# One sum of second-layer weights moved five slots earlier and one fold of keys one slot later, in a fused attention and mixture kernel

## The chip, the cores and the metric

The kernel runs on one core of one Trainium2 chip. The metric is device time in microseconds. Before the change the first three runs gave a median of 497.9 us (497.85 to 498.71).

Names: PE is the matmul engine and PEld its weight loads, DVE the vector engine, ACT the scalar engine, POOL the GpSimd engine, SP the queue that starts transfers. "L637" is line 637 of the kernel. SBUF and PSUM are the two on-chip memories that the kernel's tiles live in: the products of PE are written to PSUM tiles (in banks), nearly everything else here is in SBUF. Of the tiles, kp holds pooled keys, x_tok the attention output that is fed to the experts, acc the accumulated result, H the hidden values and S sums of them, w_bf weights, wt_bf sums of second-layer weights; unit and o_ps are PE's products in PSUM of the first and the second layer.

## The reference

Pooled attention for 8 batches, followed by a layer of four experts whose outputs are mixed by given probabilities:

```python
def _attn_ref(q, k, v):                      # 8 batches, 8 heads, 576 rows, 64 wide
    k_p = k.reshape(B, H, Sp, pool, D).mean(axis=3)       # 576 rows pooled to 72
    v_p = v.reshape(B, H, Sp, pool, D).mean(axis=3)
    ...                                                   # softmax(q k_p^T) v_p

def _moe_ref(x, domain_probs, w1, w2):       # x: 4608 x 512, 4 experts, 1024 hidden
    p = domain_probs / (domain_probs.sum(-1, keepdims=True) + 1e-09)
    for e in range(E):
        h = np.maximum(x @ w1[e], 0.0)
        out += p[:, e:e + 1] * (h @ w2[e])
```

## The kernel before

The tokens go through the experts in nine chunks. Each expert's two matrix products use seven block products in place of eight, and pay for that with sums and differences of blocks (weights, inputs, hidden values) on the DVE. The main loop is a software pipeline of slots, seven to each pair of chunk and expert. A slot is two up-products of four matmuls and one down-product of eight, and a small piece of the attention of a later batch. Everything that the change touches is hand-placed by slot number:

```python
def combine(dst, a, op, b):                       # L242: DVE, both inputs in SBUF
    nc.vector.tensor_tensor(out=dst, in0=a, in1=b, op=op)

def fold_keys(b, hs):                             # two adds per batch, L285: both inputs in SBUF
    ...
    for dup in range(2):
        nc.vector.tensor_add(out=kp_all[0:SP, hs, dup, :], in0=raw[:, hs, 0, :],
                             in1=raw[:, hs, 1, :])

def relu_sum(dst, ps, part):                      # L637: one input in PSUM, one in SBUF
    nc.vector._custom_dve(TENSOR_ADD_SAT, out=dst, in0=ps, in1=part, s0=LARGEST, s1=0.0)

def weight_sums(e):                               # the sums of second-layer weights
    ...
            lambda: combine(b12, b22, ALU.subtract, b12)]      # the fourth: the one that moves

def up_product(c, e, unit, step):
    ...                                           # four matmuls into units[unit][bank]
    if step == 0:
        nc.scalar.copy(out=units[unit][1][:], in_=ps)          # L669, ACT
    ...
    else:
        relu_sum(quarter(1, 0), ps, part[:, 0])                # L637, frees units[unit][1]

def down(c, e, step, flip=0, pooled=()):
    ...                                           # eight matmuls into a PSUM bank
    if step == 0:
        nc.scalar.copy(...)                                    # L732, ACT
    elif step in pooled and e > 0:                # step 4 alone
        ...                                                    # L736, ACT: addend = prob * product
        nc.gpsimd.tensor_add(out=dst, in0=dst, in1=addend[:])  # L738, POOL: both inputs in SBUF
    else:
        ...                                       # add: L799, DVE, one input in PSUM

# the main loop
for g in range(7 * N + 1):
    ...
    up_product(*order[t], 0, i)
    ...
    up_product(*order[t2], 1, i2)
    ...
    down(*below_of[t2], i2, t2 % 2, POOLED)
    for piece in later.get(g, ()):    # attention of later batches
        piece()
    for piece in sums.get(g, ()):     # weight sums
        piece()
```

The last up-step (L637) reads a PSUM bank that the copy L669 of the next expert's first step must overwrite, and the next up-product of PE grows on what L669 copied. So a late L637 makes L669 late, and that can stop PE.

The softmax here doesn't subtract the row's maximum and nothing guards it: scores larger than these inputs give would overflow.

Of the kernel before, what the change touches and what calls it, by code (L numbers as in the profile page):

```python
# [17 lines left out]
def kernel(  # L18
# [24 lines left out]
    BUSY = 2  # L43
# [149 lines left out]
    def load_q_rem(b):  # L193
        if b % 2 == 0:
            q_rems[b // 2] = qpool.tile([P, H, D], BF16, name="q_rem", bufs=2)
        lo = (b % 2) * REM
        nc.gpsimd.dma_start(
            out=q_rems[b // 2][lo:lo + REM],
            in_=q[b, :, NT:S, :].rearrange("h p d -> p h d"),
        )  # L200
# [40 lines left out]
    def combine(dst, a, op, b):  # L241
        nc.vector.tensor_tensor(out=dst, in0=a, in1=b, op=op)  # L242
# [28 lines left out]
    def fold_wide(what, part):  # L271
        raw, wide = ((raw_k, wide_k), (raw_v, wide_v))[what]
        a, *others = (wide[:, :, 2 * i:2 * i + 2, :] for i in range(wide.shape[2] // 2))
        if part == 0:
            for other in others:
                nc.vector.tensor_add(out=a, in0=a, in1=other)
        else:
            nc.vector.tensor_add(out=raw[:], in0=raw[:], in1=a)

    def fold_keys(b, hs):  # L280
        raw = raw_k if b >= BUSY else raws[("kraw", b)]
        if b < BUSY:
            fold(raw, hs)
# [3 lines that stand above are left out]
# [320 lines left out]
    def weight_parts(e):  # L607
        w = w1_bf[:, e]
        return w[:, 0:HK, 0:FH], w[:, HK:KC, 0:FH], w[:, 0:HK, FH:F], w[:, HK:KC, FH:F]

    def first_weight_sums(e):
        b11, b21, b12, b22 = weight_parts(e)
        t = wu_bf[:, e]
        return [lambda: combine(t[:, 0], b12, ALU.subtract, b11),
                lambda: combine(t[:, 1], b22, ALU.subtract, t[:, 0]),
                lambda: combine(t[:, 2], b21, ALU.subtract, t[:, 1]),
                lambda: combine(b12, b22, ALU.subtract, b12)]
# [13 lines left out]
    def x_sum(c, n):  # L631
        if n == 0:
            state[("x_sums", c)] = x_sums(c)
        state[("x_sums", c)][n]()
# [48 lines left out]
    def weight_sums(e):  # L683
        w, t = w2_bf[:, e], wt_bf[:, e]
        b11, b12 = w[:, LO, 0:HD], w[:, LO, HD:DM]
        b21, b22 = w[:, HI, 0:HD], w[:, HI, HD:DM]
        return [lambda: combine(t[:, 0], b12, ALU.subtract, b11),
                lambda: combine(t[:, 1], b22, ALU.subtract, t[:, 0]),
                lambda: combine(t[:, 2], b21, ALU.subtract, t[:, 1]),
                lambda: combine(b12, b22, ALU.subtract, b12)]  # L690
# [214 lines left out]
    def pieces_later():  # L905


        at = {}

        def put(slot, *pieces):  # L910
            at.setdefault(slot, []).extend(pieces)

        usual = dict(
            queries=-8, keys=-9, values=-2, scores=(-1, 3, 5, 6), contexts=(11, 14, 18, 21),
            q=1, k=(-2, 0, 5, 9), v=(-2, 0, 5, 9), x=(22, 25, 25, 25), rem=(-3, 17, 24, 25),
        )
        plans = {b: usual for b in range(BUSY, B + 1)}
        plans[BUSY] = dict(
            queries=0, keys=4, values=12, scores=(11, 12, 13, 15), contexts=(16, 18, 19, 21),
            q=6, k=(5, 8, 11, 14), v=(13, 16, 19, 24), x=(24, 25, 25, 25), rem=(0, 6, 8, 14),  # L920
        )
        plans[B] = dict(usual, x=(24, 24, 25, 25), rem=(-3, 17, 21, 22))
        plans[BUSY + 1] = dict(usual, values=4, v=(5, 8, 12, 16))

        for b, plan in plans.items():
            start = 7 * E * (b - BUSY)

            def put_each(what, pieces):
                for slot, piece in zip(plan[what], pieces, strict=True):
                    put(start + slot, piece)  # L930

            if b == BUSY:
                put(start + 1, lambda: fold_wide(0, 0))
                put(start + 4, lambda: fold_wide(0, 1))
                put(start + 5, lambda: load_q_rem(BUSY))
                put(start + 8, lambda: fold_wide(1, 0))
                put(start + 12, lambda: fold_wide(1, 1))
            if b < B:
                put(start + plan["queries"], lambda b=b: queries(b))
                put(start + plan["keys"], lambda b=b: fold_keys(b, every))  # L940
                put(start + plan["keys"] + (b > BUSY), lambda b=b: keys(b, every))
                put(start + plan["values"], lambda b=b: fold_values(b, every))
                put_each("scores", [lambda b=b, pair=pair: scores(b, pair) for pair in range(NPAIR)])

                for r, slot in zip((2, 3, 0, 1), plan["contexts"]):
                    put(start + slot, lambda b=b, r=r: context(b, r))
                    put(start + slot + 1, lambda b=b, r=r: turn(b, r))
            if b + 1 < B:
                put(start + plan["q"], lambda b=b: load_q(b + 1), lambda b=b: load_q_rem(b + 1))
                for what in range(2):  # L950
                    put_each("kv"[what], [lambda b=b, what=what, part=part: load_part(b + 1, what, part)
                                          for part in range(NR)])
            if b % 2 == 0:
                i = b // 2 - 1
                put_each("rem", [lambda i=i, do=do: do(i)
                                 for do in (rem_queries, rem_scores, rem_context, rem_turn)])
            put_each("x", [lambda b=b, n=n: x_sum(b, n) for n in range(4)])
        return at

    ENG = mybir.EngineType  # L960
    with tc.manual_schedule(
            engines={ENG.PE, ENG.DVE, ENG.Activation, ENG.Pool, ENG.SP}):
        load_q(0, 0)
        load_q(0, 1)
        load_whole(0, k, "kraw", groups(0)[:1])
        load_whole(0, k, "kraw", groups(0)[1:])
        make_identity(nc, ident[:])
        choose_rows()
        load_values_first()
        load_w1(0)  # L970
        load_w1(1)
        load_probs()
        load_w1(2)
        load_w2(0)
        load_w1(3)
        attention_first()
        norm_probs()
        load_whole(1, k, "kraw")
        load_q(1)
        load_whole(1, v, "vraw")  # L980
        load_w2(1)
        load_w2(2)
        load_w2(3)
        first_chunk()
        psum_first.__exit__(None, None, None)
        psum_last = ctx.enter_context(
            tc.tile_pool(name="psum_last", bufs=1, space=bass.MemoryType.PSUM))
        units[0] = [psum_last.tile([P, NT], F32, name=f"unit0{i}") for i in range(2)]
        open_bank(units[0][1][:])



        N = len(order)
        later = pieces_later()
        below_of = [(0, 3)] + order
        sums = {}
        for at, pieces in (((3,), weight_sums(3)[3:]), ((7,), first_weight_sums(2)[3:]), ((8,), weight_sums(1)[3:]), ((12, 15, 22, 19), weight_sums(2)),
                           ((15,), first_weight_sums(3)[3:])):
            for slot, piece in zip(at, pieces, strict=True):
                sums.setdefault(slot, []).append(piece)  # L1000
        POOLED = (4,)
        for g in range(7 * N + 1):
            t, i = divmod(g, 7)
            if i in (0, 2, 3) and t < N:
                hidden_sums(*below_of[t], i)
            if t < N:
                up_product(*order[t], 0, i)
            t2, i2 = divmod(g - 1, 7)
            if 0 <= t2 < N:
                up_product(*order[t2], 1, i2)  # L1010
            if i == 1 and t < N:
                hidden_sums(*below_of[t], i)
            if g == 0:

                down_plain(0, 2, NR - 1)
            else:
                down(*below_of[t2], i2, t2 % 2, POOLED)
            for piece in later.get(g, ()):
                piece()
            for piece in sums.get(g, ()):  # L1020
                piece()
            if g == 7 * (N - 2):
                load_last_weights()
        down_last(*order[-1])
# [28 lines left out]
```

## Time and profile before

| | before |
|---|---|
| median of the first three runs | 497.9 us |
| span of the profiled run | 495.8 us |
| PE busy | 488.6 us, 99% |
| PEld busy | 407.1 us, 82% |
| DVE busy | 377.1 us, 76% |

The Trainium skill, "Perfetto Trace Analysis", section "Identifying the Most-Contended Engine", warns that the matmuls' busy share is a poor measure of headroom, because matmuls are pipelined, and prefers MFU (the share of peak arithmetic) and the weight loads' busy share. The latter is 82% here, so 99% must not be read as "nothing to gain". What says that PE is the bound is the chain of waits (95% PE) together with a short list of things that PE ever waited for. From the page of the kernel before:

```profile
span 495.8 us, 11453 instructions
...
PE 95%; DVE 2%; ACT 1%; issue 1%; ACTq 0%
```

PE's waits (who waited for whom: us in total, times, longest):

```profile
PE unit L332 <- DVE H L818: 1.3, 1, 1.3
PE unit L656 <- ACT unit L669: 0.8, 1, 0.8
PE o_ps L297 <- ACT kp L313: 0.2, 1, 0.2
```

The first and third are in the start-up. The second is the only one in the main loop, and the ACT instruction named in it had itself waited, by the list of ACT's waits from 100 to 122 us:

```profile
ACT unit L669 <- DVE H L637: 2.4, 1, 2.4
```

The timeline around it, engine by engine (start, duration, engine, line, operation, out<-in, count, and in brackets the idle time before and what ended it). DVE:

```profile
101.29 0.68 DVE L242 TENSOR_TENSOR H<-H 128x1024 bf16<-128x1024 bf16 x1
102.74 0.88 DVE L799 SCALAR_TENSOR_TENSOR acc<-o_ps,p_all,acc 128x256 f32<-128x256 f32 x2 [0.77 <-ACT partial L671]
...
108.95 0.69 DVE L398 TENSOR_TENSOR x_tok<-att,inv 128x512 bf16<-128x512 f32 x1
109.56 1.74 DVE L285 TENSOR_TENSOR kp<-kraw 72x512 bf16<-72x512 bf16 x2
111.23 0.68 DVE L242 TENSOR_TENSOR w_bf<-w_bf 128x1024 bf16<-128x1024 bf16 x1
111.83 0.67 DVE L637 CUSTOM_DVE_ANT_0 H<-unit,partial 128x512 bf16<-128x512 f32 x1
112.43 0.85 DVE L799 SCALAR_TENSOR_TENSOR acc<-o_ps,p_all,acc 128x256 f32<-128x256 f32 x2
```

POOL, then ACT, then PE:

```profile
109.42 1.26 POOL L738 TENSOR_TENSOR acc<-acc,addend 128x512 f32<-128x512 f32 x1 [4.13 <-ACT addend L736]
```

```profile
112.59 0.57 ACT L669 COPY unit<-unit 128x512 f32<-128x512 f32 x1 [2.41 <-DVE H L637]
...
115.36 0.57 ACT L732 COPY o_ps<-o_ps 128x512 f32<-128x512 f32 x1 [0.21 <-DVE acc L799]
```

```profile
112.00 0.42 PE L435 MATMUL att<-vp,expT 72*128 72x65 bf16 x8
113.21 1.03 PE L656 MATMUL unit<-xT,w_bf 128*128 128x256 bf16 x8 [0.79 <-ACT unit L669]
```

Read from the bottom: PE stops at about 112.27 and goes on at 113.21, because L669 ran at 112.59, because L637 ran at 111.83. Yet L637's product was ready at about 109.1. In between stood the two kp adds and the weight sum. The kp adds are normally 0.41 us each; here both together took 1.74, as the list of the kp tile shows (minimum/median/maximum in ns):

```profile
L285 DVE TENSOR_TENSOR kp<-kraw x12: 408/414/1409, 81.1 to 318.5; 72x512 bf16<-72x512 bf16 x12
```

The long one, 1.409 us, is the first of the pair at 109.56. It ended at 110.97, 0.29 us after the pool add (109.42 to 110.68).

### The profile page before, as it was taken

What the parts mean: (1) busy time and instruction counts of PE and PEld (TensorE: products, weight loads), DVE (VectorE), ACT (ScalarE), POOL (GpSimd) and SP (SyncE); (2) the same over time, 40 slices, a digit from 0 to 9 for tenths busy, and PEclk for the clock granted to TensorE, in tenths of its full rate; (3) what the DMA queues carried; (4) which work ended last, traced back from release to release, by engine and by line L of the source; (5) the groups of instructions that cost most, each with busy time, mean ns of one, the idle gap of its engine ahead of it and who ended that gap; (6) DMA issues with size and microseconds to landing.
All of it is one profiled execution on the core that took longest, in us unless ns stands there. A gap on an engine that the chain in (4) does not pass through costs nothing.

```text
span 495.8 us, 11453 instructions
## 1 busy us (share of the span) xinstructions
PE 488.6 (99%) x4663; PEld 407.1 (82%) x4663; DVE 377.1 (76%) x756; ACT 302.7 (61%) x561; POOL 114.4 (23%) x112
## 2 busy tenths in 40 slices
PE   8999999999999999999999999999999999999996
PEld 5856468888888888888888888888888888888885
DVE  5567889799768975788669876896679766976674
ACT  4666536865685568656775667567665566556650
POOL 8230413232352154114421262111000100011010
PEclk9999999999999999999999999999999999999999
DMA  9999996998679659553974398130211010004003
GB/s 199 210 207 203 205 164 92 119 73 97 76 112 62 95 61 146 47 78 37 156 73 67 47 138 80 36 65 22 76 23 22 22 65 1 13 22 86 1 1 85
DMA packets 101779, 41.95 MB, mean 85 GB/s; under 512 B 73808, under 2 KB 100176, under 8 KB 101728
## 3 DMA queue, kind: packets, MB, share of 16 engines
q0 software_dynamic: 56896, 22.42, 40.4%
q1 hardware_dynamic: 43728, 17.77, 17.6%
q10 hardware_dynamic: 1104, 1.05, 0.6%
q8 instruction: 36, 0.59, 0.5%
q14 instruction: 15, 0.12, 0.1%
HBM read 45.69 MB, written 9.44 MB: 111 GB/s over the span
## 4 chain that ended last, share of the span: by engine, by line
PE 95%; DVE 2%; ACT 1%; issue 1%; ACTq 0%
PE o_ps L724 40%; PE unit L656 39%; PE unit L583 5%; PE o_ps L750 3%; PE att L382 2%; PE unit L332 1%; PE unit L782 1%; PE att L435 1%; DVE acc L799 1%; PE unit L598 0%; PE unit L306 0%; DVE H L637 0%; DVE kp L285 0%; PE att L489 0%; PE att L472 0%
## 5 line engine op out<-in xcount | busy, mean ns | idle before, releaser
L799 DVE SCALAR_TENSOR_TENSOR acc<-o_ps,p_all,acc 128x256 f32<-128x256 f32 (+1 forms) x285 | 127.1, 486 | 54.3 <-PE o_ps L724 36.1
L724 PEld LDWEIGHTS <-H 128*128 128x128 bf16 x1320 | 129.1, 98 | 16.2 <-issue 0.3
L656 PEld LDWEIGHTS <-w_bf 128*128 128x128 bf16 x1024 | 97.8, 98 | 15.9 <-issue 4.5
L637 DVE CUSTOM_DVE_ANT_0 H<-unit,partial 128x512 bf16<-128x512 f32 x128 | 87.4, 685 | 25.5 <-PE unit L656 20.9
L724 PE MATMUL o_ps<-w_bf,H 128*128 128x256 bf16 x792 | 102.6, 273 | 0.0
L656 PE MATMUL unit<-xT,w_bf 128*128 128x256 bf16 x672 | 96.4, 273 | 0.8 <-ACT unit L669 0.8
L671 ACT COPY partial<-unit 128x512 f32<-128x512 f32 x128 | 72.0, 589 | 33.2 <-PE unit L656 32.9
L738 POOL TENSOR_TENSOR acc<-acc,addend 128x512 f32<-128x512 f32 x24 | 30.4, 1265 | 258.3 <-ACT addend L736 201.3
L656 PEld LDWEIGHTS <-wu_bf 128*128 128x128 bf16 x768 | 73.3, 98 | 10.0 <-issue 1.5
L656 PE MATMUL unit<-xs,wu_bf 128*128 128x256 bf16 x512 | 76.9, 273 | 0.0
L724 PE MATMUL o_ps<-wt_bf,H 128*128 128x256 bf16 x528 | 68.4, 273 | 0.0
L724 PEld LDWEIGHTS <-S 128*128 128x128 bf16 x528 | 51.7, 98 | 6.4
L677 ACT ACTIVATE H<-unit 128x512 bf16<-128x512 f32 x64 | 38.2, 597 | 29.6 <-PE unit L656 29.3
L673 ACT ACTIVATE H<-unit 128x512 bf16<-128x512 f32 x64 | 38.8, 607 | 27.0 <-PE unit L656 27.0
L669 ACT COPY unit<-unit 128x512 f32<-128x512 f32 x64 | 37.4, 584 | 17.2 <-PE unit L656 14.7
L656 PE MATMUL unit<-xs,w_bf 128*128 128x256 bf16 x256 | 38.5, 273 | 0.0
L797 ACT ACTIVATE acc<-o_ps,p_all 128x256 f32<-128x256 f32 x72 | 30.2, 471 | 12.1 <-PE o_ps L724 10.8
L151 POOL DMA_DIRECT2D vraw<-in_v_dram x20 | 29.3, 1466 | 24.1 <-DMA vraw<-in_v_dram 23.8
L151 POOL DMA_DIRECT2D kraw<-in_k_dram x20 | 25.9, 1295 | 37.4 <-DMA kraw<-in_k_dram 37.4
L724 PE MATMUL o_ps<-wt_bf,S 128*128 128x256 bf16 x264 | 34.2, 273 | 0.0
L724 PE MATMUL o_ps<-w_bf,S 128*128 128x256 bf16 x264 | 34.2, 273 | 0.0
L656 PE MATMUL unit<-xT,wu_bf 128*128 128x256 bf16 x224 | 33.6, 272 | 0.0
(148 smaller groups left out, 516.7 us busy)
## 6 DMA issues: line engine op xcount, KB each, us to landing
out_dram<-acc SPq DMA_DIRECT2D x32, 256.0 KB, 4.2
w_bf<-in_moe_w_dram POOLq DMA_DIRECT2D x7, 1024.0 KB, 23.5
q_sb<-in_q_dram POOLq DMA_DIRECT2D x7, 512.0 KB, 9.8
vraw<-in_v_dram POOLq DMA_DIRECT2D x22, 144.0 KB, 6.5
kraw<-in_k_dram POOLq DMA_DIRECT2D x21, 144.0 KB, 5.3
w_bf<-in_moe_w_dram POOLq DMA_DIRECT2D x2, 512.0 KB, 8.8
wt_bf<-in_k_dram POOLq DMA_DIRECT2D x2, 288.0 KB, 6.8
wt_bf<-in_v_dram POOLq DMA_DIRECT2D x4, 144.0 KB, 5.6
```

The lines of the kernel that those rows point to most:

```text
L151: nc.gpsimd.dma_start(out=raw[:], in_=rows_of(src, b, 2 * part, 2 * part + 2), accum_op=ALU.add if part else ALU.bypass)
L583: nc.tensor.matmul(out_ps, lhsT=w1_bf[:, e, kc, fc * P:(fc + 1) * P], rhs=xT[:, kc, at], start=(kc == 0), stop=(kc == KC - 1), skip_group_ ...
L637: nc.vector._custom_dve(TENSOR_ADD_SAT, out=dst, in0=ps, in1=part, s0=LARGEST, s1=0.0)
L656: nc.tensor.matmul(ps[:, n * HN:(n + 1) * HN], lhsT=lhs[:, kc, f:f + P], rhs=rhs[:, kc, :], start=(not grows and n == 0 and kc == 0), stop ...
L669: nc.scalar.copy(out=units[unit][1][:], in_=ps)
L671: nc.scalar.copy(out=part[:, step - 2], in_=ps)
L673: nc.scalar.activation(out=quarter(0, 0), in_=ps, func=ACT.Relu)
L677: nc.scalar.activation(out=quarter(0, 1), in_=ps, func=ACT.Relu)
L724: nc.tensor.matmul(ps[:, j], lhsT=lhs[:, i, j * P:(j + 1) * P], rhs=rhs[:, i, :], start=(not grows and i == 0 and j == 0), stop=(i == HF - 1),
L738: nc.gpsimd.tensor_add(out=dst, in0=dst, in1=addend[:])
L797: nc.scalar.activation(out=dst, in_=o_ps, func=ACT.Copy, scale=prob)
L799: nc.vector.scalar_tensor_tensor(out=dst, in0=o_ps, scalar=prob, in1=dst, op0=ALU.mult, op1=ALU.add,)
```

## The change

The intent is to take the kp adds and the weight sum from in front of that L637: the sum goes to an earlier slot, the fold of keys (and with it the transpose of the keys) to the next slot.

```diff
-        plans[BUSY + 1] = dict(usual, values=4, v=(5, 8, 12, 16))
+        plans[BUSY + 1] = dict(usual, keys=-8, values=4, v=(5, 8, 12, 16))
...
-        for at, pieces in (((3,), ...), ((8,), weight_sums(1)[3:]), ((12, 15, 22, 19), weight_sums(2)),
+        for at, pieces in (((3,), ...), ((8,), weight_sums(1)[3:]), ((12, 15, 22, 14), weight_sums(2)),
```

(The first part of the `for` line is cut.)

## The prediction

> **What bounds the kernel now.** TensorE: the page gives it 99% of the 495.8 us span at full granted clock; the chain of waits is 95% PE. The list of PE's waits names one hole in the main loop: 0.8 us, once, unit L656 behind ACT unit L669, which itself waited 2.4 us for DVE H L637. By the timeline PE could go on at about 112.27 and starts at 113.21. The chain of waits runs through DVE from 102.74 to 112.5 us.
>
> **Why that hole is there.** The eviction H L637 at 111.83 needs a product finished at about 109.1. In the DVE's order it stood behind the fold of keys (two kp adds L285, 1.41 and 0.41 us, from 109.56) and one sum of second-layer weights (w_bf L242, 0.68 us, 0.60 us pitch, at 111.23). A kp add normally takes 0.41 us (median of 12: 414 ns). Here the first runs beside the pool engine's acc add (L738, 109.42 to 110.68) and ends 0.29 us after it. The Trainium skill, "SBUF — State Buffer", section "Who interferes with whom", says that a DVE instruction with two SBUF inputs contends with a GpSimd one that reads SBUF, and the second to issue waits. This instruction agrees (1.0 us lost); L637 (0.68) and L799 (0.47), with one input in PSUM, keep their usual length beside the other pool adds.
>
> **The change.** Nothing is added or removed; only the DVE order differs (the other engines' programs are identical).
> 1. The weight sum moves to about 99.5 us, ahead of S2, and pushes what follows by 0.60 us: H<-H ends at 102.57 instead of 101.97. The next DVE op (acc L799, 102.74) waits for a PE product ending at 102.64, so its 0.77 us of idle time absorbs that. S2 is ready at 100.8; PE reads it at 103.61.
> 2. Eviction L637 runs from 109.56 to 110.24. Copy L669 starts when its PE product ends (110.86) and is done at about 111.5, before PE needs it (112.27). The hole of about 0.94 us closes.
> 3. Two acc adds follow at 110.45, then the kp adds at about 111.2, after the pool add, at 0.41 us each. S L242 comes at about 111.9 instead of 113.22: DVE is 1.3 us earlier, PE 0.94. So the 0.15 us PE wait at 115.98 (behind ACT o_ps L732, behind acc L799) should go too.
> 4. kp is ready at about 112.0; its transpose stands on the SP queue behind qT until 113.7 anyway.
>
> All of 0.94 + 0.15 us is on the chain, and PE runs tight afterwards, so it is kept: 1.0 to 1.1 us.
>
> **Prediction: 496.9 us**, 8 in 10 between 496.2 and 497.8. Faster by over 2%: 0.5%; within 2%: 99%; slower by over 2%: 0.5%.
>
> **Signs.** Right: PE's wait behind unit L669 gone; longest kp add about 0.42 us, DVE busy down about 1 us; profiled span near 494.8; idle before acc L799 at 102.74 down to 0.2. Wrong: a PE gap between 99 and 106 us, kp still near 1.4 us, or a new PE wait at 113 to 125 us.
>
> **What would make it wrong.** The kp adds hold up S L242 or the next eviction and the hole reappears a slot later; a pool add now meets another two-input DVE op; the earlier slots meet a DMA that comes at a fixed time (kraw and vraw loads) and the microsecond is eaten; or noise of 0.8 us among runs hides it.

## The result, and the profile after

| | before | after |
|---|---|---|
| median of six runs each | 497.88 us (497.30 to 498.71) | 496.41 us (496.18 to 497.24) |
| ratio | | 0.9973, interval 0.9959 to 0.9988 |
| span of the profiled run | 495.8 us | 494.5 us |
| DVE busy | 377.1 us | 376.0 us |

The ratio is the mean time of one kernel's fast runs over that of the other's of the same rounds, so not quite the ratio of the medians. The interval excludes 1.

Lines of the profile after, in the order of those before. The page:

```profile
span 494.5 us, 11445 instructions
...
PE 98%; DVE 0%; issue 0%; ACT 0%
```

(11445 against 11453 instructions is eight matmul records missing from the trace: PE has 4655 records and PEld 4663, and all 4663 weight loads are in both traces.) All of PE's waits:

```profile
PE unit L332 <- DVE H L818: 1.3, 1, 1.3
PE o_ps L297 <- ACT kp L313: 0.2, 1, 0.2
```

ACT's wait in the same stretch:

```profile
ACT unit L669 <- PE unit L656: 0.7, 1, 0.7
```

The DVE's timeline:

```profile
99.34 0.68 DVE L242 TENSOR_TENSOR w_bf<-w_bf 128x1024 bf16<-128x1024 bf16 x1
...
101.74 0.68 DVE L242 TENSOR_TENSOR H<-H 128x1024 bf16<-128x1024 bf16 x1
102.59 0.88 DVE L799 SCALAR_TENSOR_TENSOR acc<-o_ps,p_all,acc 128x256 f32<-128x256 f32 x2 [0.17 <-ACT partial L671]
...
109.41 0.68 DVE L637 CUSTOM_DVE_ANT_0 H<-unit,partial 128x512 bf16<-128x512 f32 x1
110.31 0.88 DVE L799 SCALAR_TENSOR_TENSOR acc<-o_ps,p_all,acc 128x256 f32<-128x256 f32 x2 [0.22 <-PE o_ps L724]
111.11 0.74 DVE L285 TENSOR_TENSOR kp<-kraw 72x512 bf16<-72x512 bf16 x2
```

POOL, ACT, PE, and the kp tile:

```profile
109.28 1.26 POOL L738 TENSOR_TENSOR acc<-acc,addend 128x512 f32<-128x512 f32 x1 [4.14 <-ACT addend L736]
```

```profile
110.75 0.57 ACT L669 COPY unit<-unit 128x512 f32<-128x512 f32 x1 [0.71 <-PE unit L656]
...
114.07 0.57 ACT L732 COPY o_ps<-o_ps 128x512 f32<-128x512 f32 x1 [0.16 <-PE o_ps L724]
```

```profile
111.86 0.42 PE L435 MATMUL att<-vp,expT 72*128 72x65 bf16 x8
112.12 1.04 PE L656 MATMUL unit<-xT,w_bf 128*128 128x256 bf16 x8
```

```profile
L285 DVE TENSOR_TENSOR kp<-kraw x12: 408/412/421, 80.9 to 317.2; 72x512 bf16<-72x512 bf16 x12
```

Now L637 is what runs beside the pool add, at its usual 0.68 us, and the kp adds come after it, both together in 0.74 us. Both ACT copies now wait for PE and not for the DVE. PE goes on 0.26 us after the start of the context product, with no hole.

**Where the microsecond is.** Total times of single runs carry noise of up to a microsecond or more (below), so I compared positions: all 4663 weight loads of PE are recorded in every trace and stand in the same order, so the n-th can be subtracted from the n-th. The difference of after minus before is a staircase: it is constant at -0.14 us from 98 to 112 us (a start-up difference), drops by 0.95 us at 113.2 us and by 0.15 us at 116.0 us, and stays at -1.24 us to the end. From 106 to 117 us that is 1.09 us. So the change itself is worth 1.09 us, in two steps, and none of it is given back. "Saved from 106 to 117 us" in the next section is this measure.

### The profile page after: what moved, and what is told of

Same layout as the page of the kernel before. It is cut to its first block, busy times and chain, and to the rows that moved or that the text cites. A ratio compares the mean times of both kernels' runs of the same rounds, so it can differ in the third digit from the quotient of the medians.

```text
span 494.5 us, 11445 instructions
## 1 busy us (share of the span) xinstructions
PE 487.8 (99%) x4655; PEld 406.9 (82%) x4663; DVE 376.0 (76%) x756; ACT 302.6 (61%) x561; POOL 114.4 (23%) x112
## 3 DMA queue, kind: packets, MB, share of 16 engines
q10 hardware_dynamic: 1104, 1.05, 0.6%
## 4 chain that ended last, share of the span: by engine, by line
PE 98%; DVE 0%; issue 0%; ACT 0%
PE o_ps L724 41%; PE unit L656 40%; PE unit L583 5%; PE o_ps L750 3%; PE att L382 2%; PE att L435 1%; PE unit L782 1%; PE unit L332 1%; PE unit L598 1%; PE unit L306 0%; PE att L489 0%; PE att L472 0%; PE att_first L435 0%; PE unit L321 0%; PE o_ps L598 0%
## 5 line engine op out<-in xcount | busy, mean ns | idle before, releaser
L799 DVE SCALAR_TENSOR_TENSOR acc<-o_ps,p_all,acc 128x256 f32<-128x256 f32 (+1 forms) x285 | 127.2, 487 | 54.1 <-PE o_ps L724 36.5
L637 DVE CUSTOM_DVE_ANT_0 H<-unit,partial 128x512 bf16<-128x512 f32 x128 | 87.5, 686 | 25.5 <-PE unit L656 20.9
L669 ACT COPY unit<-unit 128x512 f32<-128x512 f32 x64 | 37.4, 584 | 15.4 <-PE unit L656 15.4
L797 ACT ACTIVATE acc<-o_ps,p_all 128x256 f32<-128x256 f32 x72 | 30.2, 471 | 12.1 <-PE o_ps L724 11.0
```

Of the source, the lines that this page charges most:

```text
L797: nc.scalar.activation(out=dst, in_=o_ps, func=ACT.Copy, scale=prob)
L799: nc.vector.scalar_tensor_tensor(out=dst, in0=o_ps, scalar=prob, in1=dst, op0=ALU.mult, op1=ALU.add,)
```

## The experiments

Theories before the first run. **Mine:** the first kp add is held by the pool add for 1.0 us, and this is what made L637 late; any two-input DVE instruction in that place would be held. **Rival A:** the order alone; the normal lengths of the three instructions in front of L637 are enough, and the long kp add is beside the point. **Rival B:** the kp add is slow for a reason of its own, such as its data landing late.

| run | what | kp adds / sum | saved from 106 to 117 us | median, ratio to before in the same rounds |
|---|---|---|---|---|
| changed kernel | both parts | 0.41 / 0.68 | 1.09 | 496.41, 0.9973 (0.9959 to 0.9988) |
| e7_after_again | the same | 0.41 / 0.68 | 1.09 | 496.41, 0.9968 (0.9943 to 0.9994) |
| e1_sum_only | sum alone | 1.41 / 0.68 | 0.59 | 497.4, 0.9989 (0.9976 to 1.0002) |
| e6_sum_only_again | the same | 1.41 / 0.68 | 0.60 | 497.7, one run |
| e2_keys_only | keys alone | 0.41 / 1.68 | 0.00 | 497.65, 0.9999 (0.9987 to 1.0011) |
| e3_pool_later | before, pool add later | 0.41 / 0.68 | 1.00 | 496.99, 0.9987 (0.9969 to 1.0006) |
| e4_sum_17 | both, sum in slot 17 | 0.41 / 0.68 | 0.63 | 497.61, 0.9997 (0.9983 to 1.0012) |
| e5_sum_18 | both, sum in slot 18 | 0.41 / 0.68 | 1.05 | 496.86, 0.9978 (0.9953 to 1.0004) |
| e9_sum_18_again | the same | 0.41 / 0.68 | 1.05 | 497.92, one run |
| e8_before_again | the kernel before | 1.41 / 0.68 | 0.00 | 498.3, one run |

Durations are of the first kp add at this place and of the moved weight sum, in us. All runs were correct. The timed medians roughly point the same way, but the intervals of all but the changed kernel reach 1; what follows rests on the traces. The rounds ran on different chips (e1 to e4 on chip 0, e5 to e7 on 3, e8 and e9 on 4); a ratio is always to before on the same chip.

### The sum alone: e1_sum_only

```diff
-((12, 15, 22, 19), weight_sums(2))
+((12, 15, 22, 14), weight_sums(2))
```

> Only the weight sum moves (slot 14), the fold of keys stays. My theory (the first kp add loses about 1.0 us to the pool add beside it; the DVE order then decides): kp still takes about 1.4 us; H L637 starts at about 111.2 instead of 111.83, copy L669 ends at about 112.6, so a PE hole of about 0.35 us stays before the next up-product, and the 0.15 us one before the following down-product stays: about 0.6 us saved, half of the change. Rival A (the order alone: 0.6 us of weight sum plus 0.74 us of normal kp time were the whole delay, the long kp add is beside the point): most of the gain, 0.9 us, from either part. Rival B (the kp add is slow because of its own data landing): kp slow here too, as in mine.

The DVE's timeline of e1_sum_only:

```profile
110.25 1.75 DVE L285 TENSOR_TENSOR kp<-kraw 72x512 bf16<-72x512 bf16 x2
111.92 0.68 DVE L637 CUSTOM_DVE_ANT_0 H<-unit,partial 128x512 bf16<-128x512 f32 x1
```

The kp add again took 1.41 us beside the pool add. L637 started at 111.92 in a trace whose weight loads stood 0.69 us later than before's at that point, so 0.6 us earlier against PE. PE's hole shrank from 0.95 to 0.35 us, and the 0.15 us one stayed: 0.59 us saved, about as expected, and well short of rival A's 0.9. The trace also had a delay of 0.61 us at about 95 us (PE behind a scores exponential on ACT) that the changed kernel does not have; see e6 and e9.

### The fold of keys alone: e2_keys_only

```diff
-        plans[BUSY + 1] = dict(usual, values=4, v=(5, 8, 12, 16))
+        plans[BUSY + 1] = dict(usual, keys=-8, values=4, v=(5, 8, 12, 16))
```

> Only the fold of keys moves (slot 20), the weight sum stays in slot 19 and so is the first two-input DVE op beside the pool add. My theory: now the weight sum is held by the pool add and takes about 1.6 to 1.7 us instead of 0.68, kp takes 0.41; H L637 starts at about 111.2, PE hole about 0.3 us, but the DVE is then as late as before for the acc adds two slots on (kp comes before them), so a new PE hole of about 0.8 us opens before the down-product at about 115: gain between 0 and 0.3 us. Rival B (kp's own data): the weight sum takes 0.68 us, kp is slow or not wherever it stands, L637 starts at about 110.2, the hole is gone and the gain is the full 1.1 us or near. Rival A: the gain is 0.7 us or more.

The DVE's timeline, then PE's, of e2_keys_only:

```profile
109.72 1.68 DVE L242 TENSOR_TENSOR w_bf<-w_bf 128x1024 bf16<-128x1024 bf16 x1
111.33 0.68 DVE L637 CUSTOM_DVE_ANT_0 H<-unit,partial 128x512 bf16<-128x512 f32 x1
...
112.71 0.74 DVE L285 TENSOR_TENSOR kp<-kraw 72x512 bf16<-72x512 bf16 x2
```

```profile
115.36 0.60 PE L656 MATMUL unit<-xT,w_bf 128*128 128x256 bf16 x4 [0.31 <-ACT unit L669]
116.15 1.03 PE L724 MATMUL o_ps<-w_bf,H 128*128 128x256 bf16 x8 [0.19 <-ACT o_ps L732]
```

The penalty moved from the kp add to the weight sum, exactly as large: 1.68 less 0.68 is 1.0 us, like 1.41 less 0.41. PE gained 0.67 us at the first hole and lost 0.47 and 0.20 us at two new ones a slot later, since the DVE had the same total of work before those: S L242 started at 113.38 us, which less the 0.17 us of later start-up is 113.21, against 113.22 in the kernel before. Net: 0.00, the lower edge of what was expected. Rival B falls (the kp adds are fast here, another instruction is slow), and so does rival A for this part, which asked for 0.7 us or more.

### The pool add later, DVE order as before: e3_pool_later

```diff
-            nc.gpsimd.tensor_add(out=dst, in0=dst, in1=addend[:])
+            (held.append if (c, e) == (1, 1) else lambda do: do())(lambda: nc.gpsimd.tensor_add(...))
...
-            for piece in sums.get(g, ()):
+            for piece in (*sums.get(g, ()), *held, held.clear):
```

One pool add of 24 is issued at the end of its slot, behind the next load of values on the pool engine.

> The kernel before with its DVE order untouched; only the one pool add that stood beside kp is issued behind the next load of values on the pool engine (about 113.1 instead of 109.4 us). My theory: both kp adds take 0.41 us, L637 starts at about 110.8, copy L669 ends at about 112.1, just before PE needs it; no PE wait behind L669; 0.9 to 1.1 us saved without either part of the change. Rival A (order alone): the hole stays for the larger part. Rival B (kp's data): kp stays at 1.4 us and the hole at 0.8 us; no gain.

DVE and POOL of e3_pool_later:

```profile
109.76 0.75 DVE L285 TENSOR_TENSOR kp<-kraw 72x512 bf16<-72x512 bf16 x2
110.43 0.68 DVE L242 TENSOR_TENSOR w_bf<-w_bf 128x1024 bf16<-128x1024 bf16 x1
111.03 0.68 DVE L637 CUSTOM_DVE_ANT_0 H<-unit,partial 128x512 bf16<-128x512 f32 x1
```

```profile
113.61 1.82 POOL L738 TENSOR_TENSOR acc<-acc,addend 128x512 f32<-128x512 f32 x1
```

(The pool add's recorded 1.82 us begin while the load of values, 112.77 to 114.13, was still on the engine.) With the DVE's order untouched, the hole behind L669 is gone (0.95 us saved) and 0.05 of the next 0.15 us as well. Without the held 1.0 us there is no big hole: in the order of before, without the collision, L637 is just early enough. Rival A falls. This is a second way to nearly the same gain.

### Another slot for the sum: e4_sum_17, e5_sum_18 and e9_sum_18_again

Both parts of the change, with 17 or 18 in place of 14.

> Both parts of the change, but the weight sum in slot 17 instead of 14. There the DVE has no idle time to take it up, so all DVE work up to L637 starts 0.6 us later than in the change (L637 at about 110.0 instead of 109.41). My theory: copy L669 waits for its PE product until 110.7 anyway, so PE has no hole and the time equals the changed kernel's within 0.1 us; the place is not special, any place ahead of the collision with slack will do. A rival for the placing (the 0.77 us idle is what pays for it): PE shows a new wait of a few tenths between 106 and 116 us and part of the gain is lost.

Here my expectation was wrong and the rival for the placing was right. PE of e4_sum_17:

```profile
107.33 1.04 PE L724 MATMUL o_ps<-w_bf,S 128*128 128x256 bf16 x8
108.66 0.42 PE L435 MATMUL att<-vp,expT 72*128 72x65 bf16 x8 [0.30 <-DVE x_tok L398]
```

The context product L435 needs the PSUM banks that the DVE empties with the x_tok of the context before. In the kernel before that x_tok ended at 108.16 and L435 began at 108.25: 0.09 us to spare. With the sum ahead of it the x_tok ended at 108.61, and PE's weight loads slipped by 0.46 us. I had followed the delay only to L637 and L669, not to every PE product that reads or overwrites what the delayed DVE work frees. The gain of the change then came on top: 0.95 and 0.15 less 0.46 is about the 0.63 us saved by positions.

> Both parts of the change, weight sum in slot 18. In slot 17 it cost PE 0.46 us because it pushed the x_tok of the second context past the start of the next context product, which had only 0.09 us to spare in the kernel before. In slot 18 it stands just behind that x_tok. If that reading is right: no PE wait behind x_tok, none behind copy L669, kp at 0.41 us, and PE weight loads after 116 us ahead of the kernel before by 0.95 + 0.15 = 1.1 us, counted from where they stood at 106 us, as in the change. If instead any delay of the DVE in this backlog costs PE time, a wait of 0.3 us or more shows between 106 and 116 us.

Up to 117 us this came out: no wait behind x_tok or L669, 1.05 us saved. So the slot matters by what stands behind the sum, not by its being far ahead. But from 124 to 129 us that trace lost 2.07 us: the DVE waited 3.1 us for a transposed x. The SP queue had taken 4.38 us to issue the transpose of queries ahead of it, and the x, issued at 118.02, then took 5.8 us to land. SP of e5_sum_18:

```profile
112.21 4.38 SPq L353 DMA_TRANSPOSE qT<-q_sb  x1
116.69 1.24 SPq L291 DMA_TRANSPOSE kpT<-kp  x1
118.02 1.25 SPq L449 DMA_TRANSPOSE xT<-x_tok  x1
```

> The kernel with the sum in slot 18 once more. Its first trace had what was expected up to 116 us, then lost 2.06 us from 124 to 129 us: the DVE's second x sum waited for the last transposed x, which the SP queue had started at 118.02 us because the transpose of queries before it took 4.38 us to issue instead of 2.2. Five of its six timed runs were faster than that one. If this is chance of the DMA queues, this trace shows the queries' transpose at about 2 us again, no PE wait at 124 us and 1.05 us saved at 125 us. If the slot causes it (the third transpose of x now starts 0.6 us later), the long issue and a wait of 1 to 2 us come back.

The second look had 2.23 us for that issue, no wait at 124 us, and 1.05 us saved at 125 us; and of the six timed runs of e5 the five others were 1.29 to 2.27 us faster than the one traced. So the 2.07 us came with that one run and not with the slot. The long issue is not all of it: in e9 the same x was issued at 117.82, only 0.20 us earlier on the trace's own clock, but it landed after 3.5 us (3.3 to 4.8 in the ten other traces). Why it landed late is not shown. It shows, though, what a transfer that comes late costs there.

### Repeats: e6_sum_only_again, e7_after_again, e8_before_again

> A second look at the kernel with the weight sum alone moved. In its first trace PE waited 0.6 us at about 95 us behind a scores exp on ACT, which stood behind an acc write that came 1.6 us late; the programs of all engines up to there are those of the changed kernel, which had no such wait, so I take it for a store or load that happened to land late: expected gone here, or at another size. The hole behind copy L669 stays near 0.35 us and the one before the next down-product at 0.15: 0.6 us saved between 106 and 116 us, as in the first look. If the 0.6 us at 95 us comes back in the same size, the move of the sum causes it.

The part that the change touches repeated: 0.60 us. The other delay came back too (0.50 us at about 95 us), which by what I had written would have pointed at the moved sum. But e9_sum_18_again, with the sum elsewhere, had it at 0.64 us, its twin e5_sum_18 did not, and neither trace of the changed kernel, which has the sum in the same slot, did. Where it occurred, an ACT write to acc (L797) at about 92 us ran 1.3 to 1.5 us late, and the traces put its wait (1.32 us in e1, 1.22 in e6, 1.35 in e9) down to the store of acc (out_dram). In e1 that was over 7 us before the moved sum ran, at 99.57. So it is not the move of the sum; why the store landed late in these three traces is not known.

> The changed kernel again, on this chip and in these rounds. Ratio 0.997 to 0.999 as before (1.1 us of 498 is 0.9978); in the trace no PE wait between 98 and 125 us, and 1.1 us saved between 106 and 117 us.

It repeated: 0.95 and 0.15 us saved (1.09 from 106 to 117 us), no PE wait between 98 and 125 us. The ratio 0.9968 is below the 0.997 that I gave as the lower edge; two runs of before in these rounds took 500.5 us and pull it down (without them it would be 0.9979), and with it the ratio of e5.

> The kernel before once more, for a second trace of it. Between 98 and 125 us nothing depends on where a transfer lands, so the same hole again: first kp add 1.41 us, PE waits 0.8 us once behind copy L669, and the positions of the PE weight loads agree with the first trace within 0.05 us from 106 to 125 us, apart from a constant.

The second trace of before stands 0.81 us later than the first from 20 us to the end, with no step in between: the same kp add of 1.41 us, the same hole. So what happens in the first 20 us alone moved this trace by 0.8 us. It may belong to the chip and not to chance: e9, the other trace of chip 4, was 0.84 us late at 20 us, and those of chips 0 and 3 between -0.03 and 0.33.

## Why the prediction was right

- **What bounds the kernel, and where the hole is.** Right: the only PE wait that the list has in the main loop was this one, and it is the one that went away.
- **Why the hole is there.** Right, and stronger than put: e3 shows that taking away the collision alone closes the big hole, e2 that the collision holds another two-input DVE instruction put there just as it held the kp add. The Trainium skill, "SBUF — State Buffer", section "Who interferes with whom", says that a DVE instruction with two SBUF inputs contends with a GpSimd instruction that reads SBUF, that the port pair is an exclusive lock, and that the order of issue decides which of the two is blocked. The traces agree: kp add and weight sum, both begun after the pool add, lost 1.0 us each; L637 and L799, with one input in PSUM, started inside the same pool add in the changed kernel and took 0.68 and 0.48 us. In all eleven traces 73 L637 and 442 L799 began inside a pool add, and none took over 0.68 and 0.49 us. The port itself is not visible in a trace; the rule fits everything seen.
- **Step 1, the idle time absorbs the sum.** Right: the idle time before L799 fell from 0.77 to 0.17 us. e4 shows what that spares: in slot 17, where the DVE has no idle time to take the sum up before the x_tok, it costs PE 0.46 us. It is not the only way: in slot 18 (e5, e9) nothing absorbs the sum either, but it stands behind that x_tok and costs nothing.
- **Steps 2 and 3, the two holes close.** Right in size: 0.94 and 0.15 us predicted, 0.95 and 0.15 measured. S L242 came at 111.77, 1.45 us earlier in the trace, of which 0.14 is start-up: 1.3, as put.
- **Step 4, nothing later waits.** Right for PE in both traces of the changed kernel. But the margin of the last transposed x became thin, as the transfers do not come earlier with the rest: it landed at 120.09 us and was read at 121.72 in the kernel before, 119.80 and 120.28 after, and in e7 it landed at 120.55 and the DVE idled 0.11 us for it. e5 shows that the named danger, a transfer that comes late for the work around it, costs time there.
- **The size.** 1.0 to 1.1 us were predicted and 1.09 measured by positions. The median was predicted as 496.9 us and measured as 496.41. The medians differ by 1.47 us (497.88 less 496.41), the fastest runs by 1.12 (497.30 less 496.18); the interval of the ratio allows a gain of 0.6 to 2.0 us, so the whole-run times alone would be weak support for this size. The rest of the medians' difference I take for the start-up and landing noise that the repeats show; with six runs a side it was not separated.

No version that beats both kernels came out of this: in the changed kernel the list of PE's waits has none left outside the start-up, and e3's other way saved 0.09 us less.

## What to carry to other kernels

When one instance of a repeated instruction is far longer than its median, look at what the other engines run in exactly that time before moving things about: moving the instruction away may only hand the penalty to the next one in line, as the fold of keys alone did. Beside the pool adds of this kernel, which read SBUF, vector work with one input in PSUM kept its length (L637, L799), so that is the work to place there. When work is moved to an earlier slot, follow the delay to every consumer behind it, including buffers that are freed late, since 0.09 us of spare time was all that one of them had; and when an effect is smaller than the noise of whole runs, compare the positions of the same instruction in two traces.

## What the Trainium skill lacked or had wrong

- "SBUF — State Buffer", "Who interferes with whom", says that the later instruction blocks, but gives no size for a two-input vector instruction beside a pool add. Here both lost 1.0 us: the held instruction ended 0.29 us (kp, 0.41 us long) and 0.55 us (weight sum, 0.68 us long) after the pool add's end, so about 0.12 us less than its own length. A third case is in e3: the moved pool add met S (L242) at 115.24, in its last 0.19 us, and S ended 0.56 us after it, only 0.07 us longer than usual. So what is lost depends on how much of the pool add is left. A pool add that was held by the DVE is in no trace: where it began second, it did so in the last 0.10 to 0.13 us of a kp or vp add, and took its usual 1.26 to 1.27 us.
- I found no page that gives the spread of a transpose's issue on the SP queue. For the same transpose of queries (at 111 to 113 us) ten traces show 1.93 to 2.63 us and one 4.38 us, and with the late x behind it, which took 5.8 us to land, PE lost 2.07 us.
- I found no page that gives the run-to-run spread of a kernel's start. Two traces of the same program stood 0.81 us apart from 20 us on and then ran in step to the end; whether that is the run or the chip was not separated.
